# One core, attention and a feed-forward layer: when and how the second and third batch's q and k are turned

## The chip, the cores and the metric

One core of one Trainium2 chip. The metric is the device time of one execution in microseconds; the median of several runs is compared.

## The reference

Eight batches of eight heads, 576 tokens, head size 64, all in float32. Attention keeps only the scores within tau = 0.02 of the row's largest:

```
scores = (q @ k.T) / 8                       # per batch and head
scores = where(scores >= max(scores) - tau, scores, -1e9)
attn   = exp(scores - max) / sum
x      = attn @ v                            # heads side by side: 4608 tokens x 512
h      = x @ w_in                            # 512 -> 2048
out    = max(0.01 * h, h) @ w_out            # 2048 -> 512
```

## The kernel before

**Steps.** The main loop runs over steps n = 0 to 143, 18 per batch: for each of two blocks of 256 queries and four pairs of heads two steps of 128 queries each, then two steps for the last 64 queries (the "tail") of all pairs. Step n issues, in this order on each engine's queue: the loads due (SyncE); the exponentials of step n-1 (`exps`, ScalarE, L291 to L295); the scores of step n (`scores`, TensorE, L252); the row turns due in this step (TensorE, L207); the minima of step n, which also copy the scores from PSUM to `s` (`copy_min`, VectorE, L260, two instructions); the threshold (L269, VectorE before step 28, GpSimd after it); on GpSimd the first entry of this step's list, the widening of a pair's reciprocal (L313), after which SyncE starts the DMA transpose of the weights `w` into `wT` (L321), and the other entries of the list; the copy of the second half of a row turn; the weights of step n-1 (`weights`, VectorE, L304, with `s` and `e` as inputs); the copy of the first half of a row turn; one unit of layer 1 (L391, its activation on ScalarE L393); the whole turns due; two units of layer 2 (L407); in every second step pv, the product of weights and v (L348), for the pair that ended some steps ago, and its evacuation from PSUM on VectorE (L370).

The order is written out by hand, and every engine works its queue in order. TensorE can start the scores of step n+1 only when both minima of step n have read PSUM, and cannot start a pair's scores before its q and k are turned.

**Splitting and turning q and k.** Each unit (batch, pair of heads or tail "t", q or k) is scaled by 64 and split into a high and a low float16 part: on GpSimd `split_scale` (L137), `split_high` (L143) and `split_low` (L151; two instructions of half the size for batches 0 and 1). The parts stand in one of four `half` buffers, `scaled` in one of two. Then TensorE turns them by multiplication with the identity:

- `turn` (whole, L186): 16 transposes over all 128 rows into one PSUM tile of tag h, copied by one instruction of 1024 columns (L195), or 8 transposes and 512 columns for a tail (L189).
- `turn_rows` (in row halves, L207): 16 transposes of 64 rows each, the even ones into a tile of tag pv, the odd ones into one of tag h, so that halves run side by side; two copies of 512 columns (L217), or of 256 for each tail (L213). Two tails share one call. The tile of tag pv is the one that pv (L348) also uses.

Batch 0 is turned around steps 0 to 10. Batch b is turned during the steps of batch b-1. The lists `loads_at`, `pool_at`, `turns_at` and `rows_at` say what is due in which step: with a unit turned in step n_, its scale and high part are due on GpSimd in step n_ - 3, its low part in n_ - 2. In step 1 the second pair of batch 0 (`first[4]` is q, `first[5]` is k of the next pair) is turned in the body of the loop.

Batch 1's first scores are those of step 18; pairs 1, 2 and 3 follow in steps 20, 22 and 24. Batch 2's follow from step 36.

Of the kernel before, what the change touches and what calls it, by code (L numbers as in the profile page):

```python
# [37 lines left out]
def kernel(  # L38
# [10 lines left out]
    nc = tc.nc  # L49
# [33 lines left out]
    def load_tails(b, which, engs=(nc.sync, nc.sync)):  # L83
        t = sb.tile([128, 2, 2, 64], FP32, tag="rawt", bufs=2, name="rawt")
        src = SRC[which][b, :, MAIN:S, :].rearrange("(u sh) p d -> u p sh d", u=2)
        for u in range(2):
            engs[u].dma_start(out=t[ds(64 * u, 64), :, :, :].rearrange("p s h d -> p (s h) d"), in_=src[u])
        tails[b, which] = t
# [29 lines left out]
    def turned_of(b, which):  # L118
        if (b, which) not in turned:
            turned[b, which] = sb.tile([128, 2, NP, WIDE[which]], FP16, tag=f"{which}T", bufs=2, name=f"{which}T")  # L120
        return turned[b, which]
# [49 lines left out]
    def turn(key, copy=None, bank="h"):  # L171
        copy = copy or nc.scalar.copy
        b, p, which = key
        dst, half = turned_of(b, which), halves.pop(key)
        n = 2 if p == "t" else 4
        c0 = 0 if which == "q" else 64
        if p == "t":
            c0 = MAIN if which == "q" else 0
            tp = ps.tile([128, 2, 2, 2, 64], FP16, tag=bank, bufs=2 if bank == "h" else 1, name="tp")
        else:  # L180
            tp = ps.tile([128, 2, 4, 128], FP16, tag="h", bufs=2, name="tp")
        for x in range(2):
            for t in range(n):
                for h in range(2):
                    o = tp[ds(64 * h, 64), x, :, t, :] if p == "t" else tp[ds(64 * h, 64), x, t, :]
                    nc.tensor.transpose(o, half[:, x, t, h, :], ident[:, :])  # L186
        if p == "t":
            src = tp[:, :, :, :, :].rearrange("d x u s p -> d x (u s) p")
            copy(out=dst[:, :, :, ds(c0, 64)], in_=src)  # L189
            if which == "k" and b:  # L190
                nc.gpsimd.tensor_copy(out=dst[:, :, :, 576:640], in_=dst[:, :, :, 0:64])
            elif which == "k":
                nc.vector.tensor_copy(out=dst[:, :, :, 576:640], in_=src)
        else:
            copy(out=dst[:, :, p, ds(c0, 512)], in_=tp[:, :, :, :].rearrange("d x t p -> d x (t p)"))  # L195

    def turn_rows(keys):

        tp = [ps.tile([128, 2, 4, 64], FP16, tag=("pv", "h")[r], bufs=1 + r, name="tpr") for r in range(2)]
        for i, key in enumerate(keys):  # L200
            half = halves.pop(key)
            for x in range(2):
                for t in range(2 if key[1] == "t" else 4):
                    for r in range(2):
                        rows = ds(64 * r, 64)
                        o = tp[r][:, i, 2 * x + t, :] if key[1] == "t" else tp[r][:, x, t, :]
                        nc.tensor.transpose(o, half[rows, x, t, :, :].rearrange("p h d -> p (h d)"), ident[rows, rows])  # L207
        def copy(r):
            for i, (b, p, which) in enumerate(keys):
                dst = turned_of(b, which)  # L210
                if p == "t":
                    c0 = MAIN if which == "q" else 0
                    nc.vector.tensor_copy(out=dst[:, :, ds(2 * r, 2), ds(c0, 64)],  # L213
                                          in_=tp[r][:, i, :, :].rearrange("d (x s) p -> d x s p", x=2))
                else:
                    c0 = 0 if which == "q" else 64
                    nc.vector.tensor_copy(  # L217
                        out=dst[:, :, p, ds(c0, 512)].rearrange("d x (t r p) -> d x t r p", t=4, r=2)[:, :, :, r, :],
                        in_=tp[r][:, :, :, :])
                if (p, which, r) == ("t", "k", 0):  # L220
                    nc.gpsimd.tensor_copy(out=dst[:, :, :, 576:640], in_=dst[:, :, :, 0:64])

        return copy
# [84 lines left out]
    def recip(pr, c, n):  # L308
        pr.rec = sb.tile([128, 2, 2], FP32, tag="rec", bufs=2, name="rec")
        nc.vector.reciprocal(out=pr.rec[:, 0:n, :], in_=pr.sum[:, ds(c, n), :])  # L310
# [118 lines left out]
    loads_at, turns_at, pool_at = {}, {}, {}  # L429

    def at(d, n, f):
        d.setdefault(n, []).append(f)

    def units(b):
        u = [(b, p, w_) for p in range(NP) for w_ in "kq"]
        return u[:2] + [(b, "t", "k")] + u[2:] + [(b, "t", "q")]

    rows_at = {}
    ROWS = [(0, "k"), (0, "q"), ("t", "k"), ("t", "q")] + [(p, w_) for p in (1, 2, 3) for w_ in "kq"]
    for b in range(1, B):  # L440
        base = PERB * (b - 1)
        for i, (s, w_) in enumerate(((0, "k"), (0, "q"), (1, "k"), (1, "q"))):
            at(loads_at, base + ((-2, 0, 5, 7)[i] if b > 1 else (3, 4, 8, 9)[i]),
               lambda b=b, s=s, w_=w_: load_main(b, s, w_))
        for i, w_ in enumerate("kq"):
            at(loads_at, base + (1, 3)[i] if b > 1 else (6, 16)[i], lambda b=b, w_=w_: load_tails(b, w_))
        for i, key in enumerate(units(b) if b == 1 else ROWS):
            n_ = base + (5, 7, 9, 9, 11, 13, 15, 17, 19, 21)[i]
            if b == 1:
                n_ = (11, 12, 14, 15, 17, 18, 19, 20, 21, 22)[i]  # L450
            key = (b,) + key[-2:]
            at(pool_at, n_ - 3, lambda key=key: split_scale(key))
            at(pool_at, n_ - 3, lambda key=key: split_high(key))
            at(pool_at, n_ - 2, lambda key=key: split_low(key))
            if b == 1:
                at(turns_at, n_, lambda key=key, i=i: turn(key, nc.vector.tensor_copy if i < 7 else None))
            else:
                at(rows_at, n_, key)
    for b in range(B):
        base = PERB * (b - 1)  # L460
# [57 lines left out]
    first = units(0)  # L518
# [24 lines left out]
    n = 0  # L543
    while n < N + 7 or l1q or l2q or stores:
        for f in loads_at.get(n, []):
            f()
        if 1 <= n <= N:
            exps(steps[n - 1])
        if n < N:
            scores(steps[n])  # L550
            turned_now = turn_rows(rows_at[n]) if n in rows_at else None
            copy_min(steps[n])
            if ended:
                recip(ended[0], 0, 2)
            if n == 5:
                turn(first[8], nc.vector.tensor_copy)
        if n == 0:
            threshold(steps[0])
        if n == 1:
            split_high_act(first[6])  # L560
            split_scale(first[6])
            split_low(first[6])
            turn(first[4], nc.vector.tensor_copy)
        if n < 11 and (n < 5 or n % 2 == 0):
            idle(8 if n else 16)
        todo = pool_at.get(n, [])
        for f in todo[:1]:
            f()
        if 0 < n < N:
            threshold(steps[n])  # L570
        if ended:
            widen(ended[0], 0, 2)
            turn_w(ended.pop())
        if n in rows_at:
            turned_now(1)
        for f in todo[1:]:
            f()
        if 1 <= n <= N:
            last = steps[n - 1]
            weights(last)  # L580
            if last.early:
                recip(last.pair, last.c, 1)
                widen(last.pair, last.c, 1, nc.vector if n < 7 else nc.gpsimd)
            elif last.c == 1 and n < 2 * PERB:

                ended.append(last.pair)
            elif last.c == 1:
                recip(last.pair, 0, last.pair.n)
                widen(last.pair, 0, last.pair.n)
                turn_w(last.pair)  # L590
        if n in rows_at:
            turned_now(0)
        while stores:
            store()
        if l1q and l1q[0][3] <= n:
            layer1()
        for f in turns_at.get(n, []):
            f()
        if 2 <= n < N + 2 and steps[n - 2].early:
            turn_w_pe(steps[n - 2].pair, steps[n - 2].c)  # L600
        for _ in range(2):
            if l2q:
                layer2(n)
        if 5 <= n < 11 and n % 2:
            idle(8)
        if n in pv_at:
            pv(pv_at[n])
            evacuate(pv_at[n], n)
        n += 1
# [33 lines left out]
```

## Time and profile before

| | us |
|---|---|
| median of 3 runs | 492.61 (492.58 to 492.98) |
| profiled execution, whole time | 492.28 |
| its span, first to last instruction | 490.3 |
| TensorE busy in the span | 475.4 (97%) |
| ScalarE busy | 432.7 (88%) |
| VectorE busy | 406.9 (83%) |
| GpSimd busy | 315.2 (64%) |
| granted TensorE clock | 1.000 of full |

The rows of the profile give start and duration in us, the engine (PE is TensorE, PEld its weight loads, DVE VectorE, ACT ScalarE, POOL GpSimd, SP SyncE), the line of the kernel, the operation, what it writes and reads with the sizes, the count, and in brackets the idle time before it with what ended it. Where a duration overlaps the next start, the distance between starts is the time that the engine gave to the instruction.

### The profile page before, as it was taken

Reading aid. Unit: us, or ns where it says so; the run is one execution under the profiler, and the core shown is the slowest. Engines: PE = TensorE matmul, PEld = TensorE weight load, DVE = VectorE, ACT = ScalarE, POOL = GpSimd, SP = SyncE. Lnnn points to the kernel's source line nnn. Section 1 sums busy time; section 2 is a strip of 40 time slices with the busy share of each in tenths; the row PEclk is TensorE's granted clock in tenths of the full one; section 3 lists DMA queues with packets and bytes.
Section 4 is the critical chain, followed back from the end, with each engine's and each line's share of the span. In section 5 each row is a group of like instructions: output and inputs, shape, how many; then the busy total and the mean of one; then the engine's idle time right before and its main releaser. Section 6 shows DMA issues by size and latency. Waiting matters only on the chain.

```text
span 490.3 us, 19692 instructions
## 1 busy us (share of the span) xinstructions
PE 475.4 (97%) x8039; PEld 343.6 (70%) x8039; DVE 406.9 (83%) x1217; ACT 432.7 (88%) x784; POOL 315.2 (64%) x534
## 2 busy tenths in 40 slices
PE   8989899999999999999999999999999999999996
PEld 6656666766777777777777777777777777667884
DVE  5999998989989899989899898989899898888100
ACT  6899999899999999999999999999999999999431
POOL 5987799678866686768766686768766673222000
PEclk9999999999999999999999999999999999999999
DMA  8999898989999998999997998999999978768412
GB/s 253 263 206 158 164 204 134 246 168 198 214 190 181 194 233 171 192 190 213 150 221 171 208 199 193 192 172 228 157 211 163 208 128 168 136 116 152 108 45 66
DMA packets 220443, 87.79 MB, mean 179 GB/s; under 512 B 190656, under 2 KB 217280, under 8 KB 220352
## 3 DMA queue, kind: packets, MB, share of 16 engines
q1 hardware_dynamic: 217120, 82.00, 81.8%
q0 software_dynamic: 2688, 4.19, 4.9%
q8 instruction: 63, 1.03, 0.9%
q10 hardware_dynamic: 544, 0.33, 0.2%
q14 instruction: 28, 0.23, 0.2%
HBM read 36.70 MB, written 9.44 MB: 94 GB/s over the span
## 4 chain that ended last, share of the span: by engine, by line
PE 78%; DVE 9%; ACT 4%; POOL 4%; DMA 2%; issue 2%; SPq 0%; POOLq 0%; DVEq 0%; ACTq 0%
PE hp L391 25%; PE o L407 20%; PE sc L252 20%; PE pv L348 7%; DVE s L260 5%; PE osc L407 4%; PE tpr L207 3%; DVE w L304 2%; POOL half L151 1%; DMA wT<-w 1%; DMA raw<-in_q_dram 1%; ACT w L292 1%; ACT e L295 1%; ACT s L291 1%; DVE x L370 1%
## 5 line engine op out<-in xcount | busy, mean ns | idle before, releaser
L260 DVE TENSOR_SCALAR_CACHE_REDUCE s<-sc 128x576 f32<-128x576 f32 x288 | 206.4, 753 | 33.4 <-PE sc L252 31.4
L252 PE MATMUL sc<-kT,qT 64*128 64x288 f16 (+1 forms) x1920 | 135.9, 285 | 4.2 <-DVE s L260 3.1
L391 PE MATMUL hp<-x,win 128*64 128x256 f16 x2048 | 136.7, 275 | 0.5 <-DVE x L370 0.5
L391 PEld LDWEIGHTS <-win 128*64 128x64 f16 x2560 | 118.5, 109 | 23.5 <-issue 17.4
L407 PE MATMUL o<-wout,g 128*64 128x512 f16 x992 | 127.8, 379 | 0.0
L304 DVE SCALAR_TENSOR_TENSOR w<-s,th,e 128x576 f16<-128x576 f32 x144 | 120.3, 835 | 0.5 <-ACT e L295 0.5
L272 POOL TENSOR_SCALAR th<-mn 128x2 f32<-128x2 f32 x116 | 52.7, 454 | 103.0 <-DVE s L260 81.2
L252 PEld LDWEIGHTS <-qT 64*128 64x128 f16 (+1 forms) x1920 | 77.0, 96 | 58.8 <-issue 43.6
L292 ACT ACTIVATE w<-s,minus_tau 128x576 f16<-128x576 f32 x144 | 111.7, 775 | 5.2
L291 ACT ACTIVATE s<-s,th 128x576 f32<-128x576 f32 x144 | 110.3, 766 | 1.9 <-POOL th L272 1.5
L295 ACT ACTIVATE e<-s,mn 128x576 f16<-128x576 f32 x144 | 110.2, 765 | 0.8 <-DVE s L260 0.8
L393 ACT ACTIVATE g<-hp 128x512 f16<-128x512 f32 x144 | 83.9, 583 | 26.2 <-PE hp L391 26.0
L151 POOL TENSOR_TENSOR half<-scaled,half 128x512 f16<-128x512 f32 (+1 forms) x91 | 89.3, 987 | 2.3
L407 PEld LDWEIGHTS <-g 128*64 128x64 f16 x1152 | 65.2, 110 | 29.8 <-issue 0.2
L348 PE MATMUL pv<-wT,v 128*64 128x256 f16 (+1 forms) x960 | 52.0, 247 | 0.5 <-DMA wT<-w 0.5
L348 PEld LDWEIGHTS <-v 128*64 128x64 f16 x960 | 41.6, 111 | 13.8 <-DMA wT<-w 1.2
L143 POOL CAST half<-scaled 128x512 f16<-128x512 f32 (+1 forms) x74 | 44.6, 602 | 4.5
L137 POOL TENSOR_SCALAR scaled<-raw 128x512 f32<-128x512 f32 x62 | 43.6, 702 | 5.4 <-DMA raw<-in_k_dram 4.4
L313 POOL CAST w<-rec 128x256 f16<-128x256 f32 (+1 forms) x70 | 32.0, 457 | 13.3 <-DVE rec L310 7.5
L106 POOL CAST v<-vraw 128x256 f16<-128x256 f32 x64 | 32.2, 532 | 1.3
L370 DVE TENSOR_TENSOR x<-pv,wT 128x256 f16<-128x256 f32 x64 | 27.1, 423 | 4.1 <-PE pv L348 4.0
L292 ACT ACTIVATION_READ_ACCUMULATOR w<-s,minus_tau 128x1 f32 x144 | 26.9, 187 | 0.0
(55 smaller groups left out, 323.1 us busy)
## 6 DMA issues: line engine op xcount, KB each, us to landing
vraw<-in_v_dram SPq DMA_DIRECT2D x16, 512.0 KB, 5.6
out_dram<-osb SPq DMA_DIRECT2D x16, 512.0 KB, 3.4
raw<-in_k_dram SPq DMA_DIRECT2D x14, 512.0 KB, 4.8
raw<-in_q_dram SPq DMA_DIRECT2D x14, 512.0 KB, 4.9
win<-in_moe_w_in_dram POOLq DMA_DIRECT2D x4, 512.0 KB, 7.3
wout<-in_moe_w_out_dram POOLq DMA_DIRECT2D x4, 512.0 KB, 13.8
wT<-w SPq DMA_TRANSPOSE x68, 5.9
raw<-in_k_dram SPq DMA_DIRECT2D x4, 256.0 KB, 5.0
```

Source lines behind the costliest of these rows:

```text
L151: nc.gpsimd.tensor_tensor(out=halves[key][:, 1, i : i + m, :, :], in0=src[:, i : i + m, :, :], in1=halves[key][:, 0, i : i + m, :, :], op= ...
L252: nc.tensor.matmul(out=o, lhsT=lhs, rhs=turned[st.b, "k"][rows, kx, pair, ds(key0, 288)], start=(i == 0), stop=(i == 2), skip_group_check= ...
L260: nc.vector.tensor_scalar(out=st.s[:, h, :].rearrange("p (a b) -> p a b", a=2), in0=st.sc[h][:, :, 0:288], scalar1=-1.0 / UNIT, scalar2=No ...
L272: nc.gpsimd.tensor_scalar(out=st.th[:, :, 0], in0=st.mn[:, :, 0], scalar1=1.0, scalar2=tau_f, op0=AX.mult, op1=AX.add)
L291: nc.scalar.activation(out=z, in_=z, func=AF.Prelu, bias=st.th[:, h, 0:1], scale=-1.0, alpha=1e20)
L292: nc.scalar.activation(out=st.w[h], in_=z, func=AF.Exp, bias=minus_tau[:, :], scale=1.0, accum_out=st.sum[h])
L295: nc.scalar.activation(out=st.e[:, :], in_=st.s[:, h, :], func=AF.Exp, bias=st.mn[:, h, 0:1], scale=-1.0)
L304: nc.vector.scalar_tensor_tensor(out=st.w[0], in0=st.s[:, 0, :], scalar=st.th[:, 0, 0:1], in1=st.e[:, :], op0=AX.is_le, op1=AX.mult, accum ...
L348: nc.tensor.matmul(out=o, lhsT=v16[st.b % 2][:, 2 * c + u if st.tail else st.p, blk, :], rhs=rhs, start=(i == 0), stop=(i == 4), skip_grou ...
L391: nc.tensor.matmul(out=hp[ds(64 * u2, 64), jj, :], lhsT=w_in16[:, i, ds(128 * j + 64 * u2, 64)], rhs=g.x[:, i, :], start=(i == 0), stop=(i ...
L393: nc.scalar.activation(out=g.g[:, ds(nj * u, nj), :], in_=hp[:, :, :], func=AF.Prelu, bias=0.0, scale=1.0, alpha=0.01)
L407: nc.tensor.matmul(out=g.o[ds(64 * u2, 64), :], lhsT=g.g[:, j, ds(128 * m + 64 * u2, 64)], rhs=w_out16[:, j, :], start=(j == 0), stop=(j = ...
```

## The change

- Batch 1's units come in the order of the later batches (both tails after pair 0), and are turned in steps 11, 12, 13, 13, 14, 15, 17, 19, 21, 23 instead of 11, 12, 14, 15, 17, 18, 19, 20, 21, 22. Those of steps 11, 12 and 14 (k and q of pair 0, k of pair 1) are turned whole, with the copy on VectorE; the others in row halves. Before, all of batch 1 was turned whole, the last three copied by ScalarE.
- In steps 21 and 23 (k and q of pair 3) the copy of the second row half is ScalarE's.
- Batch 2's k and q of pair 0 are turned in steps 25 and 27 instead of 23 and 25, its tails in 26 and 28, whole, instead of both in row halves in 27. The rest of it is unchanged.
- Batch 1's q tails are loaded in step 8 instead of 16.
- In step 1, the copy of the turned q of batch 0's second pair is ScalarE's instead of VectorE's.

```diff
-        def copy(r):
+        def copy(r, copy):
...
-                    nc.vector.tensor_copy(out=dst[:, :, ds(2 * r, 2), ds(c0, 64)],
-                                          in_=tp[r][:, i, :, :].rearrange("d (x s) p -> d x s p", x=2))
+                    copy(out=dst[:, :, ds(2 * r, 2), ds(c0, 64)],
+                         in_=tp[r][:, i, :, :].rearrange("d (x s) p -> d x s p", x=2))
...
-            at(loads_at, base + (1, 3)[i] if b > 1 else (6, 16)[i], lambda b=b, w_=w_: load_tails(b, w_))
-        for i, key in enumerate(units(b) if b == 1 else ROWS):
+            at(loads_at, base + (1, 3)[i] if b > 1 else (6, 8)[i], lambda b=b, w_=w_: load_tails(b, w_))
+        for i, key in enumerate(ROWS):
             n_ = base + (5, 7, 9, 9, 11, 13, 15, 17, 19, 21)[i]
-            if b == 1:
-                n_ = (11, 12, 14, 15, 17, 18, 19, 20, 21, 22)[i]
-            key = (b,) + key[-2:]
+            if b < 3:
+
+                n_ = base + ((11, 12, 13, 13, 14, 15, 17, 19, 21, 23), (7, 9, 8, 10, 11, 13, 15, 17, 19, 21))[b - 1][i]
+            key = (b,) + key
...
-            if b == 1:
-                at(turns_at, n_, lambda key=key, i=i: turn(key, nc.vector.tensor_copy if i < 7 else None))
+            if n_ % 2 == 0 or n_ == 11:
+                at(turns_at, n_, lambda key=key: turn(key, nc.vector.tensor_copy))
             else:
                 at(rows_at, n_, key)
...
-            turn(first[4], nc.vector.tensor_copy)
+            turn(first[4])
...
-            turned_now(1)
+            turned_now(1, nc.scalar.copy if 20 < n < 24 else nc.vector.tensor_copy)
...
-            turned_now(0)
+            turned_now(0, nc.vector.tensor_copy)
```

More of the change, by code (lines that the diff above doesn't have):

```diff
@@ L212, in copy @@
                     c0 = MAIN if which == "q" else 0
-                    nc.vector.tensor_copy(out=dst[:, :, ds(2 * r, 2), ds(c0, 64)],
-                                          in_=tp[r][:, i, :, :].rearrange("d (x s) p -> d x s p", x=2))
+                    copy(out=dst[:, :, ds(2 * r, 2), ds(c0, 64)],
+                         in_=tp[r][:, i, :, :].rearrange("d (x s) p -> d x s p", x=2))
                 else:
                     c0 = 0 if which == "q" else 64
-                    nc.vector.tensor_copy(
-                        out=dst[:, :, p, ds(c0, 512)].rearrange("d x (t r p) -> d x t r p", t=4, r=2)[:, :, :, r, :],
-                        in_=tp[r][:, :, :, :])
+                    copy(out=dst[:, :, p, ds(c0, 512)].rearrange("d x (t r p) -> d x t r p", t=4, r=2)[:, :, :, r, :],
+                         in_=tp[r][:, :, :, :])
                 if (p, which, r) == ("t", "k", 0):
```

## The prediction

> **What bounds the kernel now.** I read the table of stages first. "Step n" is pass n of the main loop; it starts here with VectorE's first minimum of that step (L260): step 11 at 44.15 us, 18 at 64.16, 21 at 73.47, 25 at 87.05, 30 at 101.21. The change touches step 1 and steps 8 to 30.
>
> ```profile
> 24.60:44.10 19.50, 16.48 (x278) 11.79 (x273) 18.63 (x65) 19.30 (x35) 16.24 (x28) 1.00 1.08 207
> 44.10:64.10 20.00, 17.88 (x316) 13.89 (x317) 19.74 (x68) 19.57 (x37) 15.21 (x21) 1.00 0.76 148
> 64.10:87.00 22.90, 22.16 (x389) 15.46 (x384) 20.65 (x68) 21.53 (x38) 21.65 (x36) 1.00 0.92 176
> 87.00:102.00 15.00, 14.60 (x228) 9.96 (x222) 14.77 (x52) 13.63 (x26) 10.98 (x16) 1.00 1.05 230
> 131.00:440.00 309.00, 308.93 (x5308) 221.48 (x5308) 276.72 (x800) 286.95 (x525) 206.03 (x352) 1.00 0.92 183
> ```
>
> After the window and its length come the busy times of PE, PEld, DVE, ACT, POOL. From 131 us on TensorE is full (308.93 of 309.00) and the steps are even, 3.09 us each, so whatever the change does to the first 30 steps is carried to the end unaltered. Up to 64 us and again from 87 to 102 VectorE is full; between them all engines are near full, so I asked the chain of waits what ended last there.
>
> ```profile
> 14.20 1.01 ACT kT L195
> ...
> 24.63 0.17 DVE rec L310
> ...
> 62.71 0.10 DVE rec L310
> 62.89 0.15 POOL half L151
> ...
> 79.27 6.04 DMA wT<-w
> 85.36 0.74 PE pv L348 x10
> ```
>
> ScalarE leads from 14.2 to 24.6, VectorE to 62.7, then GpSimd's splits, whose late widening (L313, 78.32) starts a DMA transpose at 79.27 that lands at 85.31, when TensorE wants it for step 24's pv. The timelines give the prices:
>
> ```profile
> 14.20 1.01 ACT L195 COPY kT<-tp 128x1024 f16<-128x1024 f16 x1 [1.57 <-PE tp L186]
> ```
> ```profile
> 12.49 0.69 DVE L195 COPY qT<-tp 128x1024 f16<-128x1024 f16 x1
> 13.16 1.26 DVE L304 SCALAR_TENSOR_TENSOR w<-s,th,e 128x576 f16<-128x576 f32 x1
> 48.59 1.15 DVE L304 SCALAR_TENSOR_TENSOR w<-s,th,e 128x576 f16<-128x576 f32 x1
> ```
> ```profile
> 12.51 1.30 POOL L151 TENSOR_TENSOR half<-scaled,half 128x256 f16<-128x256 f32 x2
> 59.72 1.82 POOL L151 TENSOR_TENSOR half<-scaled,half 128x256 f16<-128x256 f32 x2
> ```
> ```profile
> 85.36 0.74 PE L348 MATMUL pv<-wT,v 128*64 128x256 f16 x10 [0.52 <-DMA wT<-w]
> 92.77 0.41 PE L207 MATMUL tpr<-ident,half 64*128 64x64 f16 x16 [0.38 <-DVE x L370]
> ```
>
> See in them: ScalarE idles 1.57 us ahead of 14.20; w (L304) and GpSimd's two-operand work exclude each other (alone w takes 0.81 and a pair of L151 1.30; overlapped, the one that comes later takes 0.34 to 0.45, or 0.52, more); and a row turn waits for the evacuation L370, because one of its two banks is pv's.
>
> **Part 1, step 1: the copy of q, pair 1, goes to ScalarE.** VectorE loses 0.60 us (12.49 to 13.09). ScalarE is free from 12.63 to 14.20 and a 1024-column copy takes it 1.00, so the copy ends at 13.63, ahead of the scores that read it (14.09): no cost; had the gap been shorter, up to 1.00. VectorE's gain is worth nothing of itself, since ScalarE leads until 24.6 and is without a break from 14.20. But w(0) moves from 13.16 to about 12.69 and now meets the first of GpSimd's two subtractions at 12.51 (one L151 holds w off for about 0.48: 59.72 to w at 60.20), starts at 12.99 and holds until 13.73; the second subtraction, which began at 13.14, then ends 0.60 later, near 14.33 instead of 13.81 (the pair at 59.72: 1.82 against 1.30). Its turn on TensorE (waiting for it until 13.86), ScalarE's kT copy at 14.20 and everything behind come 0.52 later. Bounds: 0 (the subtraction goes first) and 0.60. I take **+0.52**.
>
> The Trainium skill, page "SBUF — State Buffer", section "Who interferes with whom", says that whichever of a VectorE instruction with two SBUF inputs and a GpSimd instruction starts first keeps the port for its whole length; the trace agrees that the later one waits, but shows w starting some 0.2 before the other's recorded end. By the full length this term would be about 0.7.
>
> **Part 2, SyncE.** Batch 1's q tails load in step 8 instead of 16. The load waits for a buffer that GpSimd frees at 31.9 (scale at 31.01, 0.88), so q's second half (issued 23.10) and v (27.44) behind it slip to about 33.5 and 34. The tail is wanted by GpSimd near 44.2; rawt lands 2.3 to 9.2 after issue, by 42.5 at the latest. The others are read after 58 and 69. The two issues (1.3) leave SyncE at 62.12, where the next wT waits for GpSimd until 65.17 anyway. Cost 0; if the tail were late, GpSimd would wait, at most 1 to 2 us with 1.4 of slack behind it.
>
> **Part 3, steps 11 to 20.** VectorE leads. Its step without turns is 2.29 (step 16, 2.62, less an evacuation, 0.33). A whole copy adds 0.60, a whole tail 0.34, a row unit 2 x 0.33, the two tails in rows 0.80 (step 27: 3.09). So step 13 goes from 2.52 to 3.09, 14 from 2.97 to 3.22, 15 and 17 from 2.89 to 2.95, 18 from 3.29 to 2.72 (there TensorE: L1, L2 and pv), 19 from 3.33 to 2.95, 20 from 2.68 to 2.62; 11, 12, 16 stay. Sum of the ten: 29.31 to 29.24. Of before, 0.34 (w at 48.59) and 0.43 (69.01) are waits for GpSimd. The first is kept in this sum, the second not; by GpSimd's new order I expect about one such wait in steps 13 to 20 (step 13's end meets the copy of kT, 17's the scale of 3k) and none to four of them (0 to 1.7): +0.15 taken. TensorE's row turn (0.33 against 0.47 for a whole one) and its wait for the evacuation of step 14, 16 or 18 stand beside VectorE; layer 1 ends about 1.3 after the step's start, 0.1 before the next scores may begin. ScalarE's g is thereby later (by 1.5 in step 15), with 3.4 us of room before the two buffers of s run out and 1.9 used. Steps 11 to 20: **+0.1**.
>
> **Part 4, steps 21 to 25.** TensorE leads. In step 21 the turn waits for the evacuation (0.35 later), costs 0.33 for 0.47 and is free of the stretched L1 (1.05): scores of 22 unchanged. Step 22 loses q's tail turn: -0.22, less 0.05 of slack: scores of 23 near 78.95 for 79.13. Now q of pair 3 is turned in step 23 and read in step 24. Its second half is the last thing in VectorE's step 23: 79.98 (start) + 1.43 (minima) + 0.12 (th) + 0.74 (w) + 0.34 (copy) + 0.1 = 82.7, while TensorE is ready at 78.95 + 0.84 + 0.33 + 0.89 + 0.97 = 81.98. It stands 0.75; ScalarE's half (0.57, after its w) is in by 81.8. So scores of 24 start at 82.75, not 82.07: +0.68. In step 24 the wait for wT goes: GpSimd does the widening of step 21 near 75 instead of 78.32, because its splits are spread, and the transpose lands by 82. 82.75 + 0.84 + 0.89 + 0.86 + 0.65 = 85.99 against 86.02. The stall has only changed its name. Sum **0.0**, bounds -1.2 (rival B) and +0.4.
>
> **Part 5, steps 25 to 28, VectorE leads again.** Batch 2's k of pair 0 leaves step 23, where TensorE led, for 25; q goes from 25 to 27; the tails come as whole turns in 26 and 28. VectorE's turn work in 25 to 28: before 0.66 + 0.80 = 1.46, after 0.66 + 0.34 + 0.66 + 0.34 = 2.00. Step 26 from 2.62 to 2.96, 27 from 3.09 to 2.95, 28 from 2.65 to 2.99. **+0.5** (0.3 to 0.6; TensorE's whole tails, 2 x 0.22, lie beside it). From step 29 the code is the same.
>
> **Sum.** 0.52 + 0.1 + 0.0 + 0.5 = +1.1. The profiled execution took 492.28 (span 490.3 and 2.0 around it), the median of the runs is 492.61; the sum of 493.4 in the first becomes 493.7 in the second. 0.2%, or 0.99 us, is what a measurement here can tell from no change, so +1.1 is slower by a hair.
>
> **Rivals.** A, the step-1 delay does not come (GpSimd's second subtraction keeps its turn): +0.6, 493.2, no change. For it: before, at 13.14, the subtraction was first and w paid 0.45. Against: w is then already waiting. B, faster: GpSimd is the real bound from 62 to 85, as the chain says, and spreading its splits frees more than a stall. That needs VectorE some 0.7 sooner relative to TensorE in steps 20 to 23, so that q's last half is there by 82.0; then part 4 loses the wait for the evacuation (0.35), the tail's 0.17 and the wait for wT (0.66) and gains none, -1.2; the wait at 48.59 goes too and none comes, so part 3 is -0.4; without the step-1 delay and with part 5 that makes -1.1: 491.5. Against: TensorE is full from 73 to 84.7, so the scores themselves set VectorE's start. C, slower still: VectorE's w meets GpSimd's scale or cast in each even step, 14 to 20, since these now follow directly on the widening: four waits of 0.43 less the 0.15 counted, +1.55, in all +2.65: 495.2. It decides if the casts start before w does, as at 48.52.
>
> **Chances.** Forecast 0.52, A 0.20, B 0.14, C 0.14. The forecast's own range is 492.9 to 494.3 (parts 3 to 5 with their bounds); some 0.6 of it lies over +0.99. Slower 0.14 + 0.33 = 0.47, same 0.19 + 0.20 = 0.39, faster 0.14. For 8 in 10 the range leaves out most of B and half of C, 0.17 in all: 491.9 to 495.0.
>
> **What would show it.** Right: L304's first at 12.7 to 13.0, L151's pair there 1.8 long, ScalarE's second 1024-column copy near 14.7; step 13 at 3.1 us; TensorE before the scores of step 24 waiting some 0.7 for VectorE's qT copy (L217 of before), and no wait of L348 for wT at step 24; steps 26 and 28 near 2.96. Wrong: kT's copy still at 14.2 (A), no wait at step 24's scores and step 25 before 86 (B), several w of 1.2 in steps 14 to 20 (C).

## The result, and the profile after

| | before | after |
|---|---|---|
| median of the runs | 492.6 us (492.33 to 493.05, 6 runs) | 494.93 us (494.75 to 495.55, 6 runs) |
| profiled execution, whole time | 492.28 us | 494.86 us |
| its span | 490.3 us | 492.9 us |

The ratio is 1.0047, with a 95% interval of 1.0035 to 1.0060: the change costs 2.33 us. The forecast was 493.7, +1.1 us.

In the code after the change, lines up to L217 keep their numbers and those used below that come later are one less: scores L251, minima L259, w L303, evacuation L369. The table of stages of after, its cuts moved along with the steps:

```profile
24.60:45.40 20.80, 17.93 (x285) 12.68 (x281) 19.24 (x67) 19.74 (x37) 17.27 (x29) 0.92 0.99 178
45.40:66.50 21.10, 18.18 (x342) 14.14 (x343) 21.00 (x74) 19.25 (x36) 18.34 (x27) 1.00 0.84 164
66.50:88.80 22.30, 20.86 (x334) 13.79 (x330) 20.20 (x68) 20.72 (x38) 17.46 (x28) 1.00 0.99 189
88.80:105.00 16.20, 15.16 (x250) 10.58 (x249) 15.86 (x52) 14.47 (x28) 12.59 (x19) 1.00 0.94 196
133.00:440.00 307.00, 307.00 (x5288) 220.30 (x5288) 275.03 (x797) 285.33 (x521) 206.51 (x353) 1.00 0.92 184
```

VectorE (third busy time) is again full from 45.4 to 66.5 (21.00 of 21.10) and from 88.8 to the end of the turns (15.86 of 16.20); time in which a w is held up counts as busy. TensorE (first) is no longer full in the third stage: 20.86 of 22.30, where it was 22.16 of 22.90. The first stage has a granted clock of 0.92 instead of 1.00. From 133 us on TensorE is full, as before.

The starts of the steps (VectorE's first minimum) say where the 2.6 us of these two executions came from. Step lengths in us; the last column is after's start less before's, at the step's begin:

```
step    before  after  start     step    before  after  start
   1     4.05    4.35   0.00       21     3.13    3.35  +1.55
   2     4.04    4.19  +0.31       22     3.55    3.35  +1.77
   4     3.68    4.26  +0.46       23     3.16    3.85  +1.57
   5     3.56    3.74  +1.04       24     3.73    3.26  +2.26
  12     3.23    2.89  +1.26       25     2.97    3.16  +1.79
  13     2.52    3.60  +0.92       26     2.62    3.40  +1.98
  14     2.97    3.21  +2.00       27     3.09    2.95  +2.76
  18     3.29    2.78  +2.38       28     2.65    3.00  +2.62
  19     3.33    2.96  +1.87       30     2.42    2.43  +2.97
```

Steps 1 to 10 give +1.26 (nearly all of it by step 5), 11 to 20 +0.29, 21 to 24 +0.24 and 25 to 29 +1.18. From step 30 the shift stays at 2.97 until 0.33 is lost between steps 112 and 127, about half of it near step 125, where one w of before had taken 1.354 (1.017 in after); at the end it is 2.64. The other kernels' traces lose 0.32 to 0.42 there too, so this stretch tells of before's one trace and not of the change.

The rows of step 1 in the timelines of GpSimd, VectorE and ScalarE:

```profile
12.44 1.81 POOL L151 TENSOR_TENSOR half<-scaled,half 128x256 f16<-128x256 f32 x2
```
```profile
12.69 1.04 DVE L303 SCALAR_TENSOR_TENSOR w<-s,th,e 128x576 f16<-128x576 f32 x1
```
```profile
12.55 0.99 ACT L195 COPY qT<-tp 128x1024 f16<-128x1024 f16 x1
14.65 1.01 ACT L195 COPY kT<-tp 128x1024 f16<-128x1024 f16 x1 [1.11 <-PE tp L186]
```

ScalarE had the place for q's copy, as argued. But w(0), with VectorE freed, starts at 12.69 inside GpSimd's pair of subtractions, the pair takes 1.81 instead of 1.30, TensorE turns k later, and kT's copy begins at 14.65 instead of 14.20.

Around step 24, the chain of waits and TensorE's timeline:

```profile
80.02 1.44 DVE w L303 x2
...
85.58 1.46 DVE s L259 x4
...
87.22 1.16 DVE w L303 x2
...
93.63 1.17 DVE w L303 x2
```
```profile
81.85 0.41 PE L207 MATMUL tpr<-ident,half 64*128 64x64 f16 x16 [0.26 <-DVE xt L359]
84.57 0.91 PE L251 MATMUL sc<-kT,qT 64*128 64x288 f16 x12 [0.45 <-DVE qT L217]
87.17 0.71 PE L347 MATMUL pv<-wT,v 128*64 128x256 f16 x10
95.52 0.41 PE L207 MATMUL tpr<-ident,half 64*128 64x64 f16 x16 [1.04 <-DVE x L369]
```

GpSimd's splits and the transpose into wT have gone from the chain: pv of step 24 (87.17) has no wait in front of it, where before it had 0.52. The scores of step 24 wait for VectorE's copy of q instead. And in the chain stand w's of 1.16 to 1.44 (without the 0.08 in which the threshold is read out), where 0.74 is the time of w alone: VectorE's w is held up by GpSimd's two-operand work in steps 22, 24 and 26.

### The profile page after: what moved, and what is told of

Its sections match the earlier page's. It is cut to its first block, busy times and chain, and to the rows that moved or that the text cites. A ratio compares the mean times of both kernels' runs of the same rounds, so it can differ in the third digit from the quotient of the medians.

```text
span 492.9 us, 19700 instructions
## 1 busy us (share of the span) xinstructions
PE 475.5 (96%) x8039; PEld 343.1 (70%) x8039; DVE 408.2 (83%) x1222; ACT 433.0 (88%) x784; POOL 317.5 (64%) x534
## 4 chain that ended last, share of the span: by engine, by line
PE 79%; DVE 5%; ACT 2%; issue 0%; DVEq 0%
PE hp L390 26%; PE o L406 20%; PE sc L251 20%; PE pv L347 7%; PE osc L406 4%; PE tpr L207 3%; DVE s L259 2%; DVE w L303 2%; DVE x L369 1%; ACT w L291 1%; ACT s L290 0%; ACT e L294 0%; ACT g L392 0%; DVE th L268 0%; DVE qT L217 0%
## 5 line engine op out<-in xcount | busy, mean ns | idle before, releaser
L259 DVE TENSOR_SCALAR_CACHE_REDUCE s<-sc 128x576 f32<-128x576 f32 x288 | 206.5, 754 | 35.3 <-PE sc L251 34.1
L251 PE MATMUL sc<-kT,qT 64*128 64x288 f16 (+1 forms) x1920 | 135.8, 286 | 3.9 <-DVE s L259 1.8
L303 DVE SCALAR_TENSOR_TENSOR w<-s,th,e 128x576 f16<-128x576 f32 x144 | 120.8, 839 | 0.5 <-ACT e L294 0.5
L251 PEld LDWEIGHTS <-qT 64*128 64x128 f16 (+1 forms) x1920 | 76.8, 97 | 58.5 <-issue 41.9
L151 POOL TENSOR_TENSOR half<-scaled,half 128x256 f16<-128x256 f32 (+1 forms) x91 | 90.2, 998 | 2.0
L137 POOL TENSOR_SCALAR scaled<-raw 128x512 f32<-128x512 f32 x62 | 44.8, 723 | 5.4 <-DMA raw<-in_k_dram 4.4
L369 DVE TENSOR_TENSOR x<-pv,wT 128x256 f16<-128x256 f32 x64 | 27.1, 423 | 3.8 <-PE pv L347 3.6
L207 PEld LDWEIGHTS <-half 64*128 64x128 f16 x944 | 21.9, 95 | 9.6 <-issue 6.4
```

The source lines that it names most:

```text
L151: nc.gpsimd.tensor_tensor(out=halves[key][:, 1, i : i + m, :, :], in0=src[:, i : i + m, :, :], in1=halves[key][:, 0, i : i + m, :, :], op= ...
L251: nc.tensor.matmul(out=o, lhsT=lhs, rhs=turned[st.b, "k"][rows, kx, pair, ds(key0, 288)], start=(i == 0), stop=(i == 2), skip_group_check= ...
L259: nc.vector.tensor_scalar(out=st.s[:, h, :].rearrange("p (a b) -> p a b", a=2), in0=st.sc[h][:, :, 0:288], scalar1=-1.0 / UNIT, scalar2=No ...
L303: nc.vector.scalar_tensor_tensor(out=st.w[0], in0=st.s[:, 0, :], scalar=st.th[:, 0, 0:1], in1=st.e[:, :], op0=AX.is_le, op1=AX.mult, accum ...
```

## The experiments

The first ones asked which part costs what, the others why. Ratios are to the kernel before in the same series, with their 95% intervals; 0.0010 is 0.49 us. The first 10 us differ by up to 1 us between executions, so traces are compared by step lengths or from step 3 on. Single runs of one kernel spread over 0.7 to 2 us. After itself was timed in the first series alone, so comparisons with it go through before, by the ratios, or through the plain medians.

**Step 1's copy put back on VectorE, all else as after.**

```diff
-            turn(first[4])
+            turn(first[4], nc.vector.tensor_copy)
```

> The changed kernel with one part undone: in step 1 the copy of the turned q is VectorE's again. Theory (the traces: step 5 starts 1.05 us later than before, step 6 1.22, because w(0) meets GpSimd's subtraction and what follows from it): about 1.2 us come back, 493.7 against 494.9; L151's pair at 12.5 is 1.30 long again, no stretch of half clock near 28 to 32 us. Rival (as predicted, the collision alone): 0.5 comes back, 494.4. Rival (the delay is made up later, by ScalarE's freedom): nothing comes back.

Measured: 494.17 us (493.58 to 494.57, 9 runs), ratio 1.0027 [1.0017, 1.0036], so about 1.0 us of the 2.33 came back. In the trace steps 3 to 11 lie at -0.12 against before with before's lengths, and the pair of subtractions is short:

```profile
12.39 1.30 POOL L151 TENSOR_TENSOR half<-scaled,half 128x256 f16<-128x256 f32 x2
```

The whole +1.26 of part 1 thus hangs on that one copy, and not on anything else in the change.

**Step 1's copy alone, all else as before.**

```diff
-            turn(first[4], nc.vector.tensor_copy)
+            turn(first[4])
```

> The kernel before with one part done: in step 1 the copy of the turned q is ScalarE's. Theory: from step 3 to step 11 the same lengths as in the changed kernel, 0.8 to 1.2 us longer than before (w(0) at 12.69 takes over 1.0, L151's pair 1.8, one stretch of half clock after TensorE's idling of over 1 us near 28), and all of it kept to the end: 493.5 to 493.9. Rival (the loss needs the other parts): within 0.3 of the kernel before.

Measured: 493.06 us (491.98 to 493.94, 11 runs), ratio 1.0012 [1.0002, 1.0021]. The profiled execution, the slowest of the eleven, shows the pair at 1.81, kT's copy at 15.11 and +1.1 us between steps 1 and 10, step 4 at 4.26 as in after. The median is only +0.56, less than was expected. The eleven executions spread over 2 us and those of before in the same series over 1.6 (491.67 to 493.30), so they do not show whether the price differs from execution to execution or is smaller without the other parts; that it depends on fractions of a microsecond at the start is a guess.

**Batch 2 as before, the rest as after.**

```diff
-            if b < 3:
-
-                n_ = base + ((11, 12, 13, 13, 14, 15, 17, 19, 21, 23), (7, 9, 8, 10, 11, 13, 15, 17, 19, 21))[b - 1][i]
+            if b == 1:
+                n_ = (11, 12, 13, 13, 14, 15, 17, 19, 21, 23)[i]
```

In this kernel and the next two, the last q of batch 1 and the first k of batch 2 are both due in step 23 and share one PSUM tile, so both destinations receive the second unit's values. The number of transposes and copies is that of a kernel with two tiles; whether its waits would be the same is not shown.

> The changed kernel with one part undone: batch 2's k and q of pair 0 are turned in steps 23 and 25 and its tails in row halves in 27, as before. Theory (1.18 us arise from step 25 to 30 in the changed kernel: 0.54 of VectorE's copies and 0.43 of a wait for GpSimd): 1.0 to 1.2 come back less what the copies cost in step 23, which now also has batch 1's last q: VectorE's end of step 23 moves 0.66 later, and with it the scores of 24. So 0.3 to 0.6 come back, 494.4. Rival (the copies alone, step 23 free): 1.2 come back, 493.7.

Measured: 494.24 us (494.14 to 495.52, 5 runs), ratio 1.0035 [1.0022, 1.0048], 0.6 us less than after, though the intervals overlap. Its trace has no growth at all from step 25 to 30, so the +1.18 there belongs to batch 2's moves. Step 23, for which 0.66 more was expected, takes 3.87 (3.85 in after): VectorE copies batch 1's q, which the scores wait for, ahead of batch 2's k. The run also shows why those moves are part of the change: with batch 1's last unit in step 23, batch 2's first unit has to leave it.

**Batch 1 alone: batch 2 as before, and step 1's copy back on VectorE.**

> The kernel before with batch 1's part alone (its order, its steps 11 to 23, row halves from 13 on, ScalarE's copies of pair 3's second halves, q tails loaded in step 8), batch 2 and step 1 as before. Theory: +0.3 in steps 11 to 20 (half of it w waiting for GpSimd), and in step 23 both the last q of batch 1 and the first k of batch 2, so the wait of step 24's scores grows by up to 0.66: +0.5 to +1.2, 493.1 to 493.8. Rival (GpSimd's relief frees the middle of 64 to 87 us): 0 to -0.7, 491.9 to 492.6.

Measured: 493.84 us (493.12 to 494.77, 11 runs), ratio 1.0021 [1.0012, 1.0030]: about 1.0 us for batch 1's new steps by themselves. Step 23 takes 3.87, as in after (3.85).

**The same with the halves of q and k of pair 3 swapped.** In steps 21 and 23 VectorE copies the half that comes first in its queue, and ScalarE the other.

```diff
-            turned_now(1, nc.scalar.copy if 20 < n < 24 else nc.vector.tensor_copy)
+            turned_now(1, nc.vector.tensor_copy)
...
-            turned_now(0, nc.vector.tensor_copy)
+            turned_now(0, nc.scalar.copy if 20 < n < 24 else nc.vector.tensor_copy)
```

> As batch 1's part alone, but in steps 21 and 23 VectorE copies the second halves, ahead of w, and ScalarE the first halves, behind its w. Theory (the last thing in VectorE's step 23 is what step 24's scores wait for): ScalarE is done with its half before VectorE was, the wait of the scores of 24 falls by 0.3 to 0.7, and so does the time against batch 1's part alone. Rival (VectorE's own length of step 23 sets step 24, whoever copies what): no difference within 0.2.

Measured: 492.88 us (492.19 to 494.01, 11 runs), ratio 1.0002 [0.9993, 1.0011], 0.96 us less than without the swap. Step 23 takes 3.20 instead of 3.87. The wait of part 4 is real, and it is a matter of the order of two copies: VectorE's copy of the half that comes last stood behind w in its queue.

**Batch 2 alone, the rest as before.**

```diff
+            if b == 2:
+                n_ = base + (7, 9, 8, 10, 11, 13, 15, 17, 19, 21)[i]
...
-            if b == 1:
+            if b == 1 or n_ % 2 == 0:
```

> The kernel before with one part done: batch 2's k and q of pair 0 are turned in steps 25 and 27 and its tails, whole, in 26 and 28. Theory (VectorE leads from step 25 on, and has 0.54 more to copy there): +0.5 from step 25 to 30, and up to 0.4 more where w meets GpSimd's work; step 23, free of 0.66 of copies, gives nothing back, since TensorE leads there: 493.1 to 493.5. Rival (what left step 23 comes back): within 0.2 of the kernel before.

Measured: 492.39 us (492.09 to 493.54, 11 runs), ratio 1.0004 [0.9995, 1.0013]. That is below what was expected and not to be told from no change (the ratio's interval is -0.2 to +0.6 us). In its trace (492.99 us) steps 25 to 28 grow by 0.61, with step 26 at 2.96, 27 at 3.12 and 28 at 2.84: the work of part 5 arrives in its predicted size. The median does not show it; with k of pair 0 gone from step 23, that step is 2.70 instead of 3.16, but step 22 before it takes 4.55, with a w of 1.77. How much of the 0.6 is regained in a typical execution stays open.

**Both engines copy q in step 1.** ScalarE as in after, and VectorE too, into a spare tile, so that w comes late again.

```diff
-            turn(first[4])
+            turn(first[4], twice)   # nc.scalar.copy(out, in_); nc.vector.tensor_copy(spare, in_)
```

> The changed kernel with one thing added: in step 1 VectorE also copies the turned q, to a tile that nobody reads, so that it is as busy as before, while ScalarE's copy stays the one that is used. Theory (the loss is w(0) meeting GpSimd's subtraction 0.5 earlier): w(0) starts at 13.1 to 13.2 again, L151's pair is 1.30 long, steps 1 to 6 have the lengths of before, and 0.8 to 1.2 come back as without the part: 493.7 to 494.2. Rival (ScalarE's copy is what costs: it delays ScalarE's chain or the scores of step 2): nothing comes back, 494.9.

Measured: 495.63 us (494.47 to 496.38, 5 runs), ratio 1.0064 [1.0051, 1.0077]. It could not decide, since VectorE's copy did not run beside ScalarE's:

```profile
13.78 0.69 DVE L230 COPY spare<-tp 128x1024 f16<-128x1024 f16 x1 [0.99 <-ACT qT L229]
```

The two readers of one PSUM tile came one after the other, and w only at 14.46. GpSimd's pair took 1.30 and kT's copy began at 13.79 all the same, but VectorE had a new delay of its own.

**VectorE filled with a minimum done twice in step 1.** This replaces the last one: ScalarE still copies q, and VectorE gets other work of a similar length.

```diff
-    for h in range(2)
+    for h in (0, 1, 1) if st.n == 1 else (0, 1)
```

> The changed kernel with one thing added: in step 1 VectorE does the second minimum twice (the same result in the same place), so that it is as busy as with the copy, 0.68 us for 0.60, while ScalarE keeps the copy. Theory (the loss of step 1 is w(0) meeting GpSimd's subtraction earlier): w(0) starts about 13.3, L151's pair in step 1 is 1.30 long, steps 1 to 6 have the lengths of before within 0.2, and 0.8 to 1.1 come back: 493.8 to 494.2. An engine that is given more to do makes the kernel faster. Rival (ScalarE's copy is what costs): nothing comes back or 0.1 is lost, 494.9 to 495.1.

Measured: 494.08 us (493.85 to 495.53, 7 runs), ratio 1.0033 [1.0022, 1.0044]. With one more VectorE instruction the kernel is 0.7 us faster than after (1.0047 less 1.0033, with intervals that overlap). GpSimd, VectorE and ScalarE in step 1:

```profile
12.37 1.30 POOL L151 TENSOR_TENSOR half<-scaled,half 128x256 f16<-128x256 f32 x2
```
```profile
13.79 1.16 DVE L303 SCALAR_TENSOR_TENSOR w<-s,th,e 128x576 f16<-128x576 f32 x1
```
```profile
14.07 1.01 ACT L195 COPY kT<-tp 128x1024 f16<-128x1024 f16 x1 [0.23 <-PE tp L186]
```

w now comes after the pair, the pair is short, and kT's copy is at 14.07. From step 1 to step 6 the shift against before goes from +0.30 to -0.08. So neither the copy on ScalarE nor the one missing on VectorE costs anything by itself: what costs is the moment at which w arrives.

**Only the halves swapped, all else as after.** The diff is the swap above.

> The changed kernel with one thing mended: in steps 21 and 23 VectorE copies the second halves, ahead of w, and ScalarE the first ones. Theory (step 24's scores wait for the last copy in VectorE's step 23): step 23 is 3.2 and not 3.85 long, and 0.7 to 0.9 come back: 494.0 to 494.2. Rival (VectorE sets the end of step 23 by itself): nothing, 494.9.

Measured: 494.16 us (493.55 to 495.01, 6 runs), ratio 1.0030 [1.0019, 1.0041], 0.77 less than after. On TensorE the scores of step 24 have nothing in front of them:

```profile
84.42 0.91 PE L251 MATMUL sc<-kT,qT 64*128 64x288 f16 x12
```

Step 23 is 3.35. From 25 to 30 the trace grows by only 0.61 (3.01, 2.97, 3.12, 2.84): with VectorE sooner, w(25) no longer meets GpSimd. That is part 5 as predicted, without its collision.

**More filling matmuls in step 5.** `idle(n)` issues n matmuls whose result nobody reads. The first stage's clock of 0.92 came from one stretch of half clock, 28.61 to 32.02 us, that begins beside an idle gap of TensorE:

```diff
-            idle(8)
+            idle(16 if n == 5 else 8)
```

> The changed kernel with one thing added: eight more multiplications by the identity in step 5, which nobody reads, so that TensorE's idle time near 27.6 to 28.8 us shrinks from 1.26 to about 0.75, its length in the kernel before. Theory (the stretch of half clock that begins there comes from that idle time): the clock stays at 1.0, step 6's scores take 0.91 and not 1.62, and 0.2 comes back, 494.7. Rival (the clock falls for another reason): the stretch stays. In the time the two can hardly be told apart, in the trace they can.

Measured: 494.73 us (493.55 to 495.36, 6 runs), ratio 1.0037 [1.0024, 1.0050]. The gap falls from 1.26 to 0.82 us and the clock stays at 1.0 in the profiled execution. But so it did with the swap alone, whose gap is as long as after's (TensorE's timelines of after, this kernel and the swap):

```profile
28.83 1.62 PE L251 MATMUL sc<-kT,qT 64*128 64x288 f16 x12 [1.26 <-DVE qT L195]
```
```profile
28.98 0.91 PE L251 MATMUL sc<-kT,qT 64*128 64x288 f16 x12 [0.82 <-DVE qT L195]
```
```profile
29.48 0.91 PE L251 MATMUL sc<-kT,qT 64*128 64x288 f16 x12 [1.26 <-DVE qT L195]
```

So the run does not show that the gap brings the half clock, and the gain against after lies within the two intervals. The stretch itself costs some 0.2 to 0.3 us where it occurs: step 5 takes 3.74 in after and 3.46 in the kernel with step 1's copy alone, which has the same delays but full clock.

**A version without the three collisions.** Step 1's copy back on VectorE, the halves swapped, and batch 1's q tail taken out of the doubly used step 13 and turned whole in step 24, after TensorE's tight steps.

```diff
-                n_ = base + ((11, 12, 13, 13, 14, ...
+                n_ = base + ((11, 12, 13, 24, 14, ...
```

> The changed kernel with three things mended: step 1's copy is VectorE's again; in steps 21 and 23 ScalarE copies the first halves and VectorE the second ones; batch 1's q tail, first needed in step 34, is turned whole in step 24 and no more in 13. Theory: step 1's part is undone (-0.8 to -1.2), the scores of 24 wait 0.7 to 0.9 less, step 13 loses 0.4 of copies and, with one unit less in GpSimd's list, the 0.5 that w waited there; step 24 gains 0.34 of VectorE's time, which TensorE covers; batch 2's +0.5 to +0.9 stays: 492.2 to 493.0, and the step 13 near 2.7. Rival (steps 12 to 24 are bound by GpSimd and only pass the wait on): 493.3 or more.

Measured: 491.83 us (491.58 to 492.71, 11 runs), ratio 0.9988 [0.9979, 0.9997]: about 0.6 us less than before, and 3 less than after. Step 13 takes 2.80 instead of 3.60, 23 takes 3.13, and 24 takes 3.48 with the tail in it. The table of stages for its steps 11 to 17:

```profile
43.40:63.80 20.40, 17.20 (x324) 13.31 (x325) 20.30 (x70) 18.45 (x35) 15.75 (x24) 1.00 0.93 179
```

VectorE is full here too (20.30 of 20.40), so what is left in this stretch is VectorE's own work and what holds it up: one w, in step 16, still meets GpSimd (1.34; that step is 3.15 for 2.62).

Where the 0.6 us against before comes from is not shown. In this trace 0.61 is gained in step 1 alone, whose code is that of before: w(0) met nothing and took 0.82, for 1.26 in before's trace. Steps 11 to 24 are 0.17 shorter than before's, 25 to 29 are 0.59 longer.

**The same, with batch 2's tails copied by ScalarE.**

```diff
-                at(turns_at, n_, lambda key=key: turn(key, nc.vector.tensor_copy))
+                at(turns_at, n_, lambda key=key: turn(key, nc.scalar.copy if key[:2] == (2, "t") else nc.vector.tensor_copy))
```

> As the version with the q tail later, the halves swapped and step 1 undone (0.9988 of the kernel before), and batch 2's tails, turned whole in steps 26 and 28, are copied by ScalarE. Theory (VectorE leads from 25 to 30, ScalarE has room: e starts 2 to 2.5 after the minima and 3.4 is the limit): VectorE loses 0.68, so 0.3 to 0.7 come back against that version: 491.2 to 491.6. Rival (ScalarE, 0.57 a copy and busy throughout in 26 to 30, becomes the bound): 0 to +0.5, 491.9 to 492.4.

Measured: 492.03 us (491.37 to 492.86, 11 runs), ratio 0.9990 [0.9981, 0.9998], no better. Steps 26 and 28 fall to 2.67 and 2.51, from 3.00 and 2.84, but 27 and 30 rise to 3.44 and 3.19, from 3.11 and 2.84: taking 0.34 us from the engine that leads moved its next instructions, and the gain was given back. In step 27 it is w again, 1.30 long for 0.97. From step 25 to step 32 both traces grow by the same 0.6 against before. Steps 11 to 24, whose edits are the same in both kernels, are 0.70 shorter than before's here (0.17 in the other), since w(15) in step 16 met nothing (0.81 for 1.34).

## Why the prediction was right, and where its sizes were off

The sign was right, with +1.1 forecast and +2.33 measured. The step-1 delay and the wait of step 24's scores came where they were named, and the wait for wT went. The 494.93 us lie above the forecast's own range (492.9 to 494.3) and 0.07 under the top of the wide one (495.0), which reached that far because it took in half of rival C; they are nearer to C's 495.2 than to the forecast's 493.7. That the wide range held is in part luck. What failed is the size of two terms, parts 1 and 5, mainly in one thing: how often VectorE and GpSimd exclude each other.

**Part 1, +0.52.** The mechanism is right, to the row: w(0) was put at 12.69 and came there, the pair took 1.81 (1.82 was used), kT's copy slipped 0.45. The kernels with the old copy and with the minimum done twice confirm it: the delay goes when w comes later, whatever makes it late. One number in it was read too boldly: the 0.48 for which one subtraction holds w off comes from a w that was not held at all (60.20 follows its threshold at once, and is 0.81 long), so it was an upper bound, and that w(0) ended at 13.73, as forecast, is partly luck. Rival A, that the delay does not come, fell in this trace and in that of step 1's copy alone; whether it holds in some of the latter's faster executions is not shown. The step that failed is "everything behind come 0.52 later". The trace adds 0.58 in step 4 and 0.18 in step 5, 1.26 in all; the runs give about 1.0 within the change and 0.56 alone. In step 4 VectorE was late for a second pair of GpSimd. The rows in after:

```profile
25.39 0.17 DVE L309 RECIPROCAL rec<-sum 128x2 f32<-128x2 f32 x1 [0.53 <-ACT w L291]
25.59 0.50 DVE L312 CAST w<-rec 128x128 f16<-128x128 f32 x1
```
```profile
24.30 1.71 POOL L151 TENSOR_TENSOR half<-scaled,half 128x256 f16<-128x256 f32 x2
```

and in before:

```profile
24.63 0.17 DVE L310 RECIPROCAL rec<-sum 128x2 f32<-128x2 f32 x1 [0.23 <-ACT w L292]
24.83 0.23 DVE L313 CAST w<-rec 128x128 f16<-128x128 f32 x1
```
```profile
23.83 1.75 POOL L151 TENSOR_TENSOR half<-scaled,half 128x256 f16<-128x256 f32 x2
```

The reciprocal is 0.76 late and the widening takes 0.50 instead of 0.23 while GpSimd's subtractions run (24.30 to 26.01). Of the 0.76, 0.45 is ScalarE's delay. The other 0.3 is not a wait for ScalarE, though the profile names it: its w ends at 25.05. In six traces (after, step 1's copy alone, batch 2 as before, both engines copying, more filling, the swap alone) the reciprocal comes 0.51 to 0.53 after the end of VectorE's own w, in two of them 0.75 and 1.19 after ScalarE was done; in all the others it comes 0.03 after ScalarE. What holds it, no run told. In step 5, the half clock adds about 0.2.

**Part 2, 0.** Right: no wait for a load of SyncE's stands in the chain.

**Part 3, +0.1; measured +0.29.** The step lengths came out as summed: 14, 15, 17 and 19 within 0.01 (3.21, 2.96, 2.95, 2.96), 18 at 2.78 for 2.72, 20 at 2.73 for 2.62. Step 13 is the exception, 3.60 for 3.09. The term "about one such wait in steps 13 to 20" is what happened, only it fell into step 13, onto the longest step:

```profile
53.14 1.32 DVE L303 SCALAR_TENSOR_TENSOR w<-s,th,e 128x576 f16<-128x576 f32 x1
```
```profile
53.17 1.82 POOL L151 TENSOR_TENSOR half<-scaled,half 128x256 f16<-128x256 f32 x2
```

That is 0.51 over 0.81, beside GpSimd's pair, which takes 1.82 for 1.30. The 0.34 and 0.43 of before both went, where the sum had kept the first. In steps 14 to 20 w mostly came first and GpSimd paid, which costs the path nothing: rival C named these steps, and there it did not decide.

**Part 4, 0.0; measured +0.24.** The exchange was as forecast: the wait for wT went (its transpose landed at 82.82, pv came at 87.17), and the scores of step 24 waited for VectorE's half of q. Step 23 took 3.85, where the prediction's own times give 3.8. The wait is recorded as 0.45 instead of 0.75, because 0.26 had been spent earlier, at the row turn of step 23, which waited for the tail's evacuation behind a late w:

```profile
79.93 1.52 DVE L303 SCALAR_TENSOR_TENSOR w<-s,th,e 128x576 f16<-128x576 f32 x1
...
87.14 1.24 DVE L303 SCALAR_TENSOR_TENSOR w<-s,th,e 128x576 f16<-128x576 f32 x1
...
93.55 1.24 DVE L303 SCALAR_TENSOR_TENSOR w<-s,th,e 128x576 f16<-128x576 f32 x1
```

Swapping the halves took the scores' wait away and gave 0.8 to 1.0 us. Rival B (faster) had seen 1.2 in this place, on another condition: not VectorE sooner, but its copies in another order.

**Part 5, +0.5; measured +1.18 in the trace.** VectorE's added work is as predicted (0.61 in the trace of batch 2 alone and in that of the swap alone). The rest comes from the rows just shown: w(23) delays the evacuation on which the row turn of step 25 waits, +0.19 in that step, and w(25) makes step 26 3.40 for 2.96, +0.43. The step that failed is the sum over VectorE's own work alone, 1.46 to 2.00, with no wait in it. The traces with the old step-1 copy and with the minimum done twice have the same 3.40 and the same +1.17 from 25 to 30. The runs are too coarse to say more: batch 2's moves cost 0.6 us within the change, by two ratios whose intervals overlap, and 0.2 alone.

**The sum.** At step 30 the trace has 2.97 where 1.1 was forecast. Of the 1.9 too little, 0.7 lie in part 1, 0.2 each in parts 3 and 4, 0.7 in part 5. About 1.3 of it are VectorE and GpSimd excluding each other: 0.27 at the widening in step 4, then the w of steps 13 and 22 (0.2 each, against what the sum had) and of steps 24 and 26 (0.62). That is rival C's mechanism, in other places than the even steps 14 to 20. The text had the price of one such wait nearly right, 0.4 to 0.5 (0.43 to 0.71 came), and counted them only where it had compared the lists of both engines. Whether w meets GpSimd depends on the phase of VectorE, and a shift of a few tenths sets that anew for the steps behind it: with the swap, w(25) met nothing. All these sizes are of one execution of each kernel; by the medians the forecast is 1.2 too little, not 1.9.

## What to carry to other kernels

An instruction taken from an engine that is not the bound was worth nothing here by itself, and it brought that engine's next instruction forward; look at what that one then meets, for here it met work of another engine that it holds up, and on whose result the bounding engine waited. Where two engines share a job, give the engine whose queue is fuller the half that comes ahead of its long instruction: the same two copies in the other order were worth 0.8 to 1.0 us. When a schedule entry is moved to another step, list what that step already holds: with two tails in it, step 13 took 3.60 us instead of 2.80. Look at the steps behind it too: without the second tail, steps 11 to 24 came out 0.5 us apart in two traces, by one w that met GpSimd in the one and not in the other.

## What the runs showed of the hardware

- Work added to an engine that was not the bound made the kernel faster: 0.7 us by the ratios, with one more minimum on VectorE.
- Where a w and GpSimd's work overlap, both can pay: 0.51 on a pair of subtractions (1.81 for 1.30), and 0.2 to 0.7 on w in after (1.04 to 1.52 for 0.81), up to 1.0 in batch 2 alone (1.77).
- TensorE's clock fell to half for 3.41 us in after (28.61 to 32.02), near an idle gap of 1.26 us. Another kernel with an equal gap kept full clock. The Trainium skill, page "TensorE: Matmul & The Clock Gate", section "What's actually happening", describes a free-running window of 3413 ns; the length of the stretch agrees, and the runs show that the same gap can be with or without it.
- Two engines that read one PSUM tile did so one after the other in this kernel, and the second waited 0.99 us. Whether the chip asks for that or only the order that the program was built with, no run told.
